# Two more spectral blocks behind the scans, tighter scan spacing in the front, and a rounding moved to GpSimd

## The chip, the cores and the metric

One core of one Trainium2 chip runs the whole kernel. The metric is the device time of one execution in microseconds (us); lower is better. TensorE (PE in the profile) multiplies matrices, VectorE (DVE), ScalarE (ACT) and GpSimd (POOL) work on whole tiles, and SyncE (SP) issues most of the DMAs. All of them run at their own pace, each in the order of its own instruction list, and wait for each other by semaphores. "PEld" is TensorE's loading of weights.

## The reference, cut to what matters

The output mixes softmax attention (32 heads of width 16) and the real part of a two-dimensional Fourier transform of the same input by a gate for each row. Shapes are 2048 rows by 512 columns, all float32.

```python
a = softmax(q @ k.T / 4) @ v            # per head, then @ wo        (32 heads of 16)
b = Cr @ (x @ Wr.T) - Ci @ (x @ Wi.T)   # Cr, Ci: 2048x2048 cosine and sine matrices
g = sigmoid((x * gate_w).sum(-1))
out = g * a + (1 - g) * b
```

## The kernel before

**Arithmetic.** Where exactness is needed, an operand is split into a rounded part and its rest (`hi`, `lo`, type float32r), and a product is three matmul pairs: hi·hi, hi·lo, lo·hi. "Pair" means that `halves_of` (L204) puts two matmuls of 64 rows on the upper and lower half of the array at the same time; a pair is the unit of the orders below (the profile counts its two matmuls singly).

**Scans.** The softmax needs the greatest score of every query before the exponentials. So every pair of heads (16 of them) is first scanned: 64 scans for each pair, 1024 in all (`TOTAL`). A scan multiplies 128 queries by 512 keys and takes the row maximum.

**Three stretches.**
1. The front. It computes the projections q, k, v, wr, wi (each 16 blocks of 12 pairs) and then spectral blocks (each 16 row tiles by three, that is 48 pairs): 16 blocks with the cosine matrix (`ph` 0), then blocks with the sine matrix (`ph` 1). Between the pairs of a product stand the first 740 scans (`FRONT`). `products` and the spectral loop call `beside()` after every pair; it adds 1/pace to a counter and puts a scan in whenever the counter reaches 1. The paces are numbers in the source, one for each part of the front: `PACE, SUMS, BESIDE, PART, SWAP`, in pairs for each scan. Scans in the front are "folded": `scan_folded` writes scores to one of four PSUM banks (L173), ScalarE copies the even ones to SBUF (`fold`, L177), and VectorE adds the odd ones to them and takes the maximum (`fold`, L179, followed by a short read of its accumulator, also L179). Two scans later the same bank is written again, so TensorE then waits if the reader is late.
2. The steps: 512 steps of 16 head pairs by 32 (`PERIODS`). Step by step TensorE computes scores (`qk`, L229: one pair of matmuls into a double bank, one into two single banks), ScalarE takes exponentials (L253 on 1024 columns, L261 twice on 512), and TensorE multiplies them with the values (`pv`, L752). Up to step 284 each step also holds one of the remaining scans. From step `MIX` = 285 on, each step holds "filling" instead (`next(fill)`): the generator `outputs()` yields the spectral blocks that the front left over, 16 steps each, three pairs a step (`spectral`); then `crosses()`, which gets the last `CROSS` = 8 blocks' worth from 14 products of 24 pairs each; then the output projection (`mix_heads`, 9 pairs for each of 16 row tiles, in four steps or in two); and the last parts. In even steps the filling stands ahead of the scores, in odd steps behind them, and both steps' value products are issued together at the end of the even step. So TensorE's order over two steps is: eight value products, scores, the filling of two steps in one piece, scores.
3. A short tail.

**The operands of `crosses()`** are formed on VectorE by `form_unit` (L982 rounds, L983 takes the rest), at steps given by offsets in the table `crossed`; each is loaded seven steps earlier by `begin_unit` on SP's queue, and every form writes over the block that the cross before used. `gather` (L1028, L1029) empties the accumulator after 24 pairs; the additions on the results are GpSimd's, and `finish` stores them.

**The first differences.** In the front, `difference` makes the sums for folded scans from key projections: GpSimd subtracts, ScalarE rounds to `dh`, GpSimd subtracts again, SP stores. `f` = 0 falls into the first 40 us, before the scans begin. `after(n, ...)` puts a call into a list that is run n pairs later, which sets its place in every engine's order.

`ROWS` says at which scan the rows of the next head pair are fetched.

Of the kernel before, what the change touches and what calls it, by code (L numbers as in the profile page):

```python
# [24 lines left out]
NB = S // P  # L25
# [6 lines left out]
PERIODS = 2 * NB  # L32
SCANS = 64
TOTAL = SCANS * NP
LATER = 10
CROSS = 8
EARLY = range(11)
PARTS = {12: 16, 11: 20}
FRONT = SCANS * len(EARLY) + sum(PARTS.values())
PACE, SUMS, BESIDE, PART, SWAP = 2.95, 3.6, 2.72, 2.11, 2.97  # L40
END_PAIR, PART_PAIR = PARTS
SEQ = [(p, i) for p in EARLY for i in range(SCANS)]
SEQ += [(p, i) for p, n in PARTS.items() for i in range(n)]
SEQ += [(p, i) for p in (PART_PAIR, 13, 14, 15, END_PAIR) for i in range(PARTS.get(p, 0), SCANS)]
ROWS = {SCANS * n + 20: p for n, p in enumerate(EARLY[1:])}
ROWS.update({SCANS * len(EARLY) - 60: END_PAIR, SCANS * len(EARLY) - 34: PART_PAIR})
NWARM = 20
MIX = TOTAL - FRONT + 1
HALVED = MIX + NB * (LATER - CROSS)
STEPS = [3, 2, 2, 3, 2, 2, 3, 2, 2, 3]  # L50
TURN = 2 * len(STEPS)
OUT = HALVED + 7 * TURN
SLOW = 5
SCANS_IN = 0
AHEAD = (30, 31, 37, 44)
TURNED = 476
# [10 lines left out]
def build(tc, xT, wqkv, wo, wrT, wiT, cr, ci, ct, gate, out):  # L67
    nc = tc.nc
    with ExitStack() as ctx:
# [200 lines left out]
        with ExitStack() as pf:  # L270
# [11 lines left out]
            def after(n, f, *args):  # L282

                count[0] += 1
                due.append((slots[0] + n, count[0], f, args))
# [75 lines left out]
            for ph, plain, pair in ((0, range(NB - 2), (NB - 2, NB - 1)), (1, range(2, NB), (0, 1))):  # L361
                split_up = [(ph, t, u) for half in range(2) for t in pair for u in (2 * half, 2 * half + 1)]
                whole = [(ph, t, u) for t in plain for u in range(NU)]
                coef += split_up + whole if ph else whole + split_up
            coef = coef[:len(coef) - NU * LATER]
            craw, ready = {}, {}
# [25 lines left out]
            with ExitStack() as px:  # L392
# [48 lines left out]
                def difference(f, c, s):  # L441

                    kept.append(s)
                    if c % 2 == 0:
                        return
                    a, b = kept
                    kept.clear()
                    hi = (ep.tile([P, 512], F32R, tag="gb", name="dh", bufs=1) if f else
                          rp.tile([P, 512], F32R, tag="raw", name="dh"))
                    lo = b.bitcast(F32R)  # L450

                    def store(i, v):
                        nc.sync.dma_start(kf_d[f][:, i, (c - 1) * 512:c * 512], v.bitcast(F32))

                    after(11, nc.gpsimd.tensor_sub, a, a, b)
                    after(16, nc.scalar.copy, hi, a)
                    after(17, nc.gpsimd.tensor_sub, lo, a, hi.bitcast(F32))
                    after(22, store, 0, hi)
                    after(25, store, 1, lo)
# [169 lines left out]
            with ExitStack() as py:  # L629
# [36 lines left out]
                for n, (ph, t, u) in enumerate(coef):  # L666
# [12 lines left out]
                    hi, lo = ready.pop(n)  # L679
# [47 lines left out]
        with ExitStack() as pa:  # L727
# [141 lines left out]

            raws, units = [], [(t, u) for t in range(NB - LATER, NB - CROSS) for u in range(NU)]  # L870
            parts = []
# [37 lines left out]
            crossed, begun, sets, kept = [], {}, {}, {}  # L909

            for n, (left, right) in enumerate(CROSSES):
                crossed += [(TURN * n + at, n, left if f is not None else right, f, u)
                            for at, f, u in ((-8, 0, 0), (-6, None, 0), (-5, None, 1), (-4, None, 2), (-2, None, 3),
                                             (-1, 0, 1), (0, None, 4), (1, None, 5), (2, None, 6), (4, None, 7),
                                             (7, 1, 0), (9, 1, 1))]

            def quarter(f, u, a, b):

# [136 lines left out]
            def crosses():  # L1055

                for n in range(len(CROSSES)):
                    for f in range(2):
                        ps = pair_banks()
                        done = 0  # L1060
                        for u in range(8):
                            left, right = sets[f, u // CS], sets[None, u]
                            q = slice((u % CS) * P, (u % CS + 1) * P)
                            for i, (a, b) in enumerate(((0, 0), (0, 1), (1, 0))):
                                halves_of((ps[:, 0, :], ps[:, 1, :]), left[a][:, q], right[b],
                                          u == 0 and i == 0, u == 7 and i == 2)
                                done += 1
                                if done in [sum(STEPS[:k]) for k in range(1, len(STEPS))]:
                                    yield
                        gather(n, f, ps, now[0] - HALVED)  # L1070
                        yield

# [50 lines left out]
            def outputs():  # L1123

                for t in range(NB - LATER, NB - CROSS):
                    yield from spectral(t)
# [46 lines left out]
            for step in range(NP * PERIODS):  # L1173
                p, i = step // PERIODS, step % PERIODS
# [38 lines left out]
                done = None  # L1213
                for _ in range(min(len(pend), 1) if step < MIX else 0 if step % 2 else 2):
                    done = flush()
# [10 lines left out]
                sum_quarters(step)  # L1226
                crossing(step - HALVED)
                if TURNED <= step < TURNED + CROSS:
                    load_turned(NB - CROSS + step - TURNED)
                if TURNED + 11 <= step < TURNED + 11 + CROSS:  # L1230
                    take_turned(NB - CROSS + step - TURNED - 11)
# [76 lines left out]
```

## Time and profile before

| | us |
|---|---|
| time, median of 3 runs (lowest, highest) | 1734.22 (1733.69, 1735.02) |
| the profiled execution | 1735.44 |
| its span, first to last instruction | 1733.6 |
| front: up to the first wide exponential | 669.4 |
| steps with scans (0 to 287, by the wide exponentials) | 550.2 |
| steps with spectral filling (288 to 319) | 69.9 |
| steps 320 to 511 and the tail | 444.1 |

The granted TensorE clock is 0.999 of full speed over the span. The rows of the profile quoted in the prediction come from five views: the page of the whole execution; windows (busy time of each engine in a stretch, with the number of instructions in brackets); groups of instructions by line in a window; and the timeline, whose rows give the start in us from the span's start, the duration, the engine, the line, what is written from what, how often in sequence, and in brackets the idle time before with the instruction that ended it; and windows for one line alone.

### The profile page before, as it was taken

To read this page: it belongs to the slowest core of one execution; us is meant where nothing else is said; L and a number is where in the kernel's file an instruction comes from. 1 tells how busy PE (TensorE), PEld (TensorE's weight loads), DVE (VectorE), ACT (ScalarE), POOL (GpSimd) and SP (SyncE) were. 2 spreads that over 40 slices of the span, in tenths; PEclk is the share of its full clock that TensorE was granted. 3 is DMA by queue.
4 is the path that set the end of the run, shared out by engine and by line. 5 is a ranking of instruction groups with operands and counts; after the bars stand their busy time and mean duration, and the time that the engine had idled before them with its cause. 6 is when DMAs were issued, how large, how long until landed. Compare 5 with 4: busy or idle time off the path is not lost.

```text
span 1733.6 us, 36853 instructions
## 1 busy us (share of the span) xinstructions
PE 1718.4 (99%) x13560; PEld 1034.1 (60%) x13560; DVE 1149.3 (66%) x2290; ACT 1540.4 (89%) x2554; POOL 744.8 (43%) x893
## 2 busy tenths in 40 slices
PE   8999999999999999999999999999999999999998
PEld 6889888998988786333333333334554444444454
DVE  6688888899999996676676676667133435353243
ACT  5788888888888888999999999999888888888886
POOL 3452234755555762434535455353322334344222
PEclk9999999999999999999999999999999999999999
DMA  7783446643435676256444445354365444455733
GB/s 272 240 318 72 129 137 198 173 117 112 123 112 164 167 160 126 72 130 166 135 110 115 117 117 142 87 140 93 101 148 127 117 115 110 130 142 139 178 108 125
DMA packets 149573, 242.04 MB, mean 140 GB/s; under 512 B 50144, under 2 KB 60880, under 8 KB 142800
## 3 DMA queue, kind: packets, MB, share of 16 engines
q1 hardware_dynamic: 134128, 218.32, 45.5%
q0 software_dynamic: 14688, 20.33, 5.0%
q8 instruction: 106, 1.74, 0.4%
q10 hardware_dynamic: 576, 1.05, 0.2%
q14 instruction: 75, 0.61, 0.1%
HBM read 156.24 MB, written 83.11 MB: 138 GB/s over the span
## 4 chain that ended last, share of the span: by engine, by line
PE 95%; DMA 2%; DVE 1%; SPq 0%; issue 0%; POOL 0%; ACT 0%; DVEq 0%; POOLq 0%; ACTq 0%
PE pvb L752 28%; PE xy L204 25%; PE s L229 19%; PE s L173 11%; PE s L204 8%; PE s L154 4%; DMA raws<-wqkv 0%; DMA q_d<-eh 0%; DMA raws<-xT 0%; DVE fold L179 0%; PE s L549 0%; DVE y L867 0%; SPq L780 0%; DMA b<-o_d 0%; DVE b L348 0%
## 5 line engine op out<-in xcount | busy, mean ns | idle before, releaser
L253 ACT ACTIVATE eb<-s 128x1024 f32<-128x1024 f32 x512 | 571.7, 1117 | 67.0 <-PE s L229 66.9
L261 ACT ACTIVATE e<-s 128x512 f32<-128x512 f32 x1022 | 602.1, 695 | 0.0
L179 DVE CUSTOM_DVE_ANT_0 fold<-s,fold 128x512 f32<-128x512 f32 x740 | 497.8, 690 | 67.7 <-PE s L173 37.2
L177 ACT ACTIVATE fold<-s 128x512 f32<-128x512 f32 x740 | 437.2, 603 | 84.9 <-PE s L173 65.8
L752 PE MATMUL pvb<-eb,va 128*17 128x512 f32 x2052 | 511.5, 597 | 0.3 <-DVE ob L761 0.3
L752 PE MATMUL pvb<-e,va 128*17 128x512 f32 x2044 | 510.7, 597 | 0.0
L156 DVE TENSOR_REDUCE mx<-s 128x2 f32<-128x1024 f32 x284 | 348.0, 1225 | 171.7 <-PE s L154 171.6
L229 PE MATMUL s<-qs,ks 50*128 50x512 f32 x2048 | 435.3, 439 | 0.0
L229 PEld LDWEIGHTS s<-qs,ks 50*128 50x128 f32 x2048 | 210.0, 184 | 371.8 <-ACT eb L253 252.1
L204 PE MATMUL xy<-b,c 64*128 64x512 f32 x2496 | 405.8, 392 | 2.5 <-DVE b L348 1.6
L173 PE MATMUL s<-ks,qs 48*128 48x512 f32 x1480 | 356.7, 403 | 1.8 <-DVE mx L179 1.3
L204 PEld LDWEIGHTS xy<-b,c 64*128 64x128 f32 x2496 | 289.4, 187 | 22.6 <-DVE b L348 2.9
L173 PEld LDWEIGHTS s<-ks,qs 48*128 48x128 f32 x1480 | 194.4, 184 | 46.0 <-DVE mx L179 10.8
L752 PEld LDWEIGHTS pvb<-eb,va 128*17 128x17 f32 x2052 | 71.3, 96 | 193.7 <-issue 184.8
L204 PE MATMUL s<-b,b 64*128 64x512 f32 x1050 | 139.8, 392 | 0.1
L204 PE MATMUL xy<-w,b 64*128 64x512 f32 x768 | 116.8, 392 | 0.0
L154 PE MATMUL s<-ks,qs 48*128 48x512 f32 x568 | 114.9, 395 | 0.1
L204 PEld LDWEIGHTS s<-b,b 64*128 64x128 f32 x1050 | 100.2, 185 | 24.5 <-issue 1.0
L379 POOL TENSOR_TENSOR c<-craw,c 128x512 fp32r<-128x512 f32 x84 | 109.1, 1298 | 6.7
L771 POOL DMA_DIRECT2D r_d<-lc x31 | 17.8, 575 | 214.5 <-DVE lc L770 194.6
L764 POOL DMA_DIRECT2D lc<-ob x124 | 62.8, 513 | 103.7 <-DVE ob L761 90.7
L773 POOL DMA_DIRECT2D rb<-r_d x124 | 60.5, 495 | 106.4 <-DMA r_d<-lc 101.0
(142 smaller groups left out, 1538.8 us busy)
## 6 DMA issues: line engine op xcount, KB each, us to landing
qs<-q_d SPq DMA_DIRECT2D x68, 256.0 KB, 5.7
craw<-cr SPq DMA_DIRECT2D x60, 256.0 KB, 3.5
craw<-ct SPq DMA_DIRECT2D x48, 256.0 KB, 4.9
ks<-k_d SPq DMA_DIRECT2D x42, 256.0 KB, 5.9
kept_None<-sum SPq DMA_DIRECT2D x40, 256.0 KB, 2.4
craw<-kept_None SPq DMA_DIRECT2D x40, 256.0 KB, 3.8
qs<-q_d SPq DMA_DIRECT2D x68, 128.0 KB, 7.1
craw<-ci SPq DMA_DIRECT2D x32, 256.0 KB, 4.3
```

Of the source, the lines that this page charges most:

```text
L154: nc.tensor.matmul(ps[:, j, :], qs[b:b + 48, qb * P:(qb + 1) * P], ks[b:b + 48, c * 512:(c + 1) * 512], start=True, stop=True)
L156: nc.vector.tensor_reduce(mx[p][:, :, qb, c], ps, axis=AX.X, op=ALU.max)
L173: nc.tensor.matmul(ps, qs[b:b + 48, qb * P:(qb + 1) * P], ks[b:b + 48, c * 512:(c + 1) * 512], start=True, stop=True)
L177: nc.scalar.activation(fold[j], ps, AF.Relu)
L179: nc.vector.tensor_tensor_reduce(out=fold[j], in0=ps, in1=fold[j], scale=1.0, scalar=-3.0e38, op0=ALU.add, op1=ALU.max, accum_out=mx[p][:, ...
L204: nc.tensor.matmul(ps[j], lhs[r], rhs[r], start=first, stop=last)
L229: nc.tensor.matmul(pss[j], ks[b:b + 50, kb * P:(kb + 1) * P], qs[b:b + 50, q0:q0 + 512], start=True, stop=True)
L253: nc.scalar.activation(e, ps, AF.Exp, scale=SCALE)
L261: nc.scalar.activation(e[j], pss[j], AF.Exp, scale=SCALE)
L379: sub(lo, raw, hi.bitcast(F32))
L752: nc.tensor.matmul(pvb[r:r + VC, :], va[:, kb, 2 * p + j, :], es[c][j], start=kb == 0, stop=kb == NB - 1, tile_position=(0, r))
L764: nc.gpsimd.dma_start(lc[32 * n:32 * n + 32, :], ob[r + DH:r + VC, :].rearrange("p (s e) -> p s e", e=16))
```

## The change

The number of sine blocks left to the steps (`LATER`) rises from 10 to 12, so the front computes two blocks fewer and `outputs()` two more (`t` = 4 and 5). The number of scans in the front stays 740, and the paces are made tighter to fit them in. To keep the total number of steps, a cross product of 24 pairs now takes 8 steps of three pairs; before it took 10 steps of 3, 2, 2, 3, 2, 2, 3, 2, 2 and 3 pairs. The offsets in `crossed` are compressed from a turn of 20 steps to one of 16. `HALVED`, the step at which the crosses begin, goes from 317 to 349, and `OUT`, where the output projection begins, from 457 to 461. `SLOW` goes from 5 to 3: three row tiles of the output projection instead of five are spread over four steps. The rows of the tenth next pair are fetched 10 scans later. The rounding of `dh` for `f` = 0 goes from ScalarE to GpSimd.

```diff
-LATER = 10
+LATER = 12
 CROSS = 8
+SAVED = 2 * CROSS
-PACE, SUMS, BESIDE, PART, SWAP = 2.95, 3.6, 2.72, 2.11, 2.97
+PACE, SUMS, BESIDE, PART, SWAP = 2.72, 3.1, 2.5, 2.03, 2.85
-ROWS = {SCANS * n + 20: p for n, p in enumerate(EARLY[1:])}
+ROWS = {SCANS * n + (20 if n < 9 else 30): p for n, p in enumerate(EARLY[1:])}
 MIX = TOTAL - FRONT + 1
+OUT = MIX + NB * LATER - SAVED
 HALVED = MIX + NB * (LATER - CROSS)
-STEPS = [3, 2, 2, 3, 2, 2, 3, 2, 2, 3]
-TURN = 2 * len(STEPS)
-OUT = HALVED + 7 * TURN
-SLOW = 5
+SLOW = 3
...
-                    after(16, nc.scalar.copy, hi, a)
+                    after(16, nc.scalar.copy if f else nc.gpsimd.tensor_copy, hi, a)
...
-                crossed += [(TURN * n + at, n, left if f is not None else right, f, u)
-                            for at, f, u in ((-8, 0, 0), (-6, None, 0), (-5, None, 1), (-4, None, 2), (-2, None, 3),
-                                             (-1, 0, 1), (0, None, 4), (1, None, 5), (2, None, 6), (4, None, 7),
-                                             (7, 1, 0), (9, 1, 1))]
+                crossed += [(NB * n + at, n, left if f is not None else right, f, u)
+                            for at, f, u in ((-8, 0, 0), (-6, None, 0), (-5, None, 1), (-4, None, 2), (-2, 0, 1),
+                                             (-1, None, 3), (0, None, 4), (2, None, 5), (3, None, 6), (4, None, 7),
+                                             (6, 1, 0), (7, 1, 1))]
...
-                        done = 0
                         for u in range(8):
...
-                                done += 1
-                                if done in [sum(STEPS[:k]) for k in range(1, len(STEPS))]:
-                                    yield
+                            if u < 7:
+                                yield
                         gather(n, f, ps, now[0] - HALVED)
                         yield
```

In the orders below the changed kernel's lines stand one lower than the old ones, `w_1220` of the old is `w_1234` of the new, and x2 is one pair.

**ScalarE and GpSimd near the end of the first key and query blocks** (about 24 to 33 us of the profile; `b` are the split columns of x that the next products read, `raws` the loaded ones, `eh` a rounded projection, `tx` an emptied accumulator). ScalarE before:

```order
L471 COPY tx<-s_469 128x512
L297 CAST dh<-s 128x512
L347 CAST b_227<-raws 128x512
L297 CAST eh<-s 128x512
L347 CAST b_229<-raws 128x512
L471 COPY tx<-xy 128x512
```

ScalarE now:

```order
L470 COPY tx<-s_469 128x512
L346 CAST b_227<-raws 128x512
L296 CAST eh<-s 128x512
L346 CAST b_229<-raws 128x512
L470 COPY tx<-xy 128x512
```

GpSimd now, where before the CAST was missing:

```order
L296 TENSOR_TENSOR el<-s,eh 128x512 x4
L296 TENSOR_TENSOR s<-s 128x512
L296 CAST dh<-s 128x512
L296 TENSOR_TENSOR s<-s,dh 128x512
L296 TENSOR_TENSOR el<-s,eh 128x512 x4
```

The rounding has left ScalarE's list, where it stood ahead of four roundings of x, and now stands between GpSimd's two subtractions.

**TensorE in the value projection** (a stretch with the pace `BESIDE`; L204 a pair of the product, L173 a scan). Before:

```order
L204 MATMUL xy<-w_1220,b_231 128x512 x2
L204 MATMUL xy<-w_1221,b_231 128x512 x2
L173 MATMUL s<-ks,qs 128x512 x2
L204 MATMUL xy<-w_1220,b_232 128x512 x2
L204 MATMUL xy<-w_1220,b_233 128x512 x2
L204 MATMUL xy<-w_1221,b_233 128x512 x2
L173 MATMUL s<-ks,qs 128x512 x2
```

Now, a little further on:

```order
L203 MATMUL xy<-w_1235,b_229 128x512 x2
L203 MATMUL xy<-w_1234,b_230 128x512 x2
L172 MATMUL s<-ks,qs 128x512 x2
L203 MATMUL xy<-w_1234,b_231 128x512 x2
L203 MATMUL xy<-w_1235,b_231 128x512 x2
L203 MATMUL xy<-w_1234,b_232 128x512 x2
L172 MATMUL s<-ks,qs 128x512 x2
L203 MATMUL xy<-w_1234,b_233 128x512 x2
L203 MATMUL xy<-w_1235,b_233 128x512 x2
L172 MATMUL s<-ks,qs 128x512 x2
```

Runs of two and three pairs between scans alternate now, where three were the rule. Over the whole front TensorE's list holds 2016 pairs and 740 scans before, 1920 pairs and 740 scans now; 71, 70 and 71 scans stand in the v, wr and wi projections before, 77 in each now.

**TensorE in the crosses** (L229 the scores of a step, L204 the filling of two steps). Before:

```order
L229 MATMUL s_18595<-qs,ks 128x512 x2
L229 MATMUL s_18599<-qs,ks 128x512
L229 MATMUL s_18600<-qs,ks 128x512
L204 MATMUL s_18419<-b_18475,b_18405 128x512 x2
L204 MATMUL s_18419<-b_18474,b_18406 128x512 x2
L204 MATMUL s_18419<-b_18523,b_18405 128x512 x2
L204 MATMUL s_18419<-b_18524,b_18405 128x512 x2
L204 MATMUL s_18419<-b_18523,b_18406 128x512 x2
L229 MATMUL s_18620<-qs,ks 128x512 x2
```

Now:

```order
L228 MATMUL s_19339<-qs,ks 128x512 x2
L228 MATMUL s_19343<-qs,ks 128x512
L228 MATMUL s_19344<-qs,ks 128x512
L203 MATMUL s_19349<-b_19189,b_19143 128x512 x2
L203 MATMUL s_19349<-b_19190,b_19143 128x512 x2
L203 MATMUL s_19349<-b_19189,b_19144 128x512 x2
L203 MATMUL s_19349<-b_19219,b_19143 128x512 x2
L203 MATMUL s_19349<-b_19220,b_19143 128x512 x2
L203 MATMUL s_19349<-b_19219,b_19144 128x512 x2
L228 MATMUL s_19368<-qs,ks 128x512 x2
```

Two steps hold four or five pairs of a cross before and six now. The number of such pieces of filling is 114 before and after; 11 of them hold nine pairs before (row tiles of the output projection in two steps), 13 now.

## The prediction

> **What bounds the kernel now.** I read the page first, then windows by stretch, then timelines inside them. The page says that TensorE is never idle, which would make every pair equally dear wherever it stands:
>
> ```profile
> PE 1718.4 (99%) x13560; PEld 1034.1 (60%) x13560; DVE 1149.3 (66%) x2290; ACT 1540.4 (89%) x2554; POOL 744.8 (43%) x893
> ```
>
> The windows (us, then busy time of PE, PEld, DVE, ACT, POOL, each with its count) tell two regimes apart: the front (v projection, part of the cosine blocks) and the steps (spectral filling; steps 320 onward up to the output projection):
>
> ```profile
> 121.40:183.50 62.10, 62.10 (x528) 56.78 (x526) 54.21 (x156) 52.55 (x99) 14.51 (x12) 1.00 0.33 88
> 420.00:460.00 40.00, 40.00 (x339) 35.29 (x337) 36.74 (x111) 33.88 (x60) 20.39 (x22) 1.00 0.36 108
> 1219.60:1289.50 69.90, 69.90 (x574) 36.68 (x572) 20.87 (x38) 62.30 (x97) 20.63 (x34) 1.00 0.50 130
> 1289.50:1594.20 304.70, 304.70 (x2339) 143.31 (x2340) 130.45 (x209) 271.26 (x419) 106.45 (x149) 1.00 0.50 125
> ```
>
> PE reads full in all four, but in the front 264 pairs stand in 62.1 us (528 matmuls, 0.235 us each pair) with weights loading 91% of the time, and in the steps weights load 47 to 52%. What the steps wait for is in the timeline of two steps with six filling pairs (TensorE, then ScalarE's wide exponentials):
>
> ```profile
> 1254.66 0.61 PE L752 MATMUL pvb<-eb,va 128*17 128x512 f32 x2
> 1256.50 0.73 PE L229 MATMUL s<-qs,ks 50*128 50x512 f32 x4
> 1257.07 0.63 PE L204 MATMUL s<-b,chi 64*128 64x512 f32 x4
> 1257.54 0.39 PE L204 MATMUL s<-b,clo 64*128 64x512 f32 x2
> 1257.77 0.62 PE L204 MATMUL s<-b,chi 64*128 64x512 f32 x4
> 1258.22 0.39 PE L204 MATMUL s<-b,clo 64*128 64x512 f32 x2
> 1258.45 0.65 PE L229 MATMUL s<-qs,ks 50*128 50x512 f32 x4
> 1254.55 1.04 ACT L253 ACTIVATE eb<-s 128x1024 f32<-128x1024 f32 x1
> 1257.04 1.03 ACT L253 ACTIVATE eb<-s 128x1024 f32<-128x1024 f32 x1 [0.47 <-PE s L229]
> 1258.92 1.04 ACT L253 ACTIVATE eb<-s 128x1024 f32<-128x1024 f32 x1
> ```
>
> The first exponential waits for the scores behind the value products (0.47 us idle), the second starts as soon as ScalarE is through. So two steps last 4.37 us: a stretch of TensorE (value products and scores, 2.49 us), then a stretch of ScalarE (1.88 us), under which the filling runs, 1257.07 to 1258.45.
>
> **The steps: three pairs in each.** The crosses had four or five pairs in two steps. Here are two steps with four:
>
> ```profile
> 1467.14 1.09 PE L204 MATMUL s<-b,b 64*128 64x512 f32 x8
> 1464.61 1.04 ACT L253 ACTIVATE eb<-s 128x1024 f32<-128x1024 f32 x1
> 1468.98 1.04 ACT L253 ACTIVATE eb<-s 128x1024 f32<-128x1024 f32 x1
> ```
>
> Again 4.37 us. Over many steps (us, ScalarE's time in L253, number of them), first three pairs a step, then 2.4 but for the last steps:
>
> ```profile
> 1219.60:1289.50 69.90, 33.09 (x32) 1.00 0.50 130
> 1289.50:1569.60 280.10, 132.64 (x128) 1.00 0.50 126
> ```
>
> 69.90/32 = 2.184 and 280.10/128 = 2.188 us a step. I therefore cost the 96 pairs that move into the steps at **0**; their cover is ScalarE's stretch. What a moved block issues besides (four loads of coefficients, a load and a store of `y` on SP, four splits and two updates on VectorE) is in the first of these windows as well, which is two such blocks: VectorE has 20.87 of 69.9 us there, and the steps are no longer for any of it. In the front the same splits were GpSimd's and the emptying ScalarE's, so both are relieved. It is just enough: nine pairs, as in the output projection, don't fit. In ScalarE's timeline there, the second step of such a two takes 2.57 us, where it took 1.88 above, and ScalarE waits for scores in it too:
>
> ```profile
> 1598.35 1.03 ACT L253 ACTIVATE eb<-s 128x1024 f32<-128x1024 f32 x1 [0.47 <-PE s L229]
> 1600.92 1.02 ACT L253 ACTIVATE eb<-s 128x1024 f32<-128x1024 f32 x1 [0.56 <-PE s L229]
> ```
>
> 0.69 us for three pairs too many, 0.23 each. If the cover were gone, the moved pairs would cost that, 22 us. The output projection has 13 such pieces of nine pairs now against 11: 2 x 0.69 = **+1.4 us**. The number of steps is the same, so nothing else is added at the end; VectorE in the crosses forms 12 operands in 35 us instead of 43.75, and from 130.45/304.7 = 43% busy comes to 54% at most. Its last operands are wanted two steps (4.4 us) after they are due, at the least.
>
> **The front: two blocks less.** What one pair takes is read where 12 stand in a row; the scans between pairs from the cosine part:
>
> ```profile
> 25.33 2.88 PE L204 MATMUL s<-b,w 64*128 64x512 f32 x24
> 399.88 0.43 PE L173 MATMUL s<-ks,qs 48*128 48x512 f32 x2
> 400.12 0.66 PE L204 MATMUL xy<-b,c 64*128 64x512 f32 x4
> 400.58 0.43 PE L173 MATMUL s<-ks,qs 48*128 48x512 f32 x2
> 400.46 0.69 DVE L179 CUSTOM_DVE_ANT_0 fold<-s,fold 128x512 f32<-128x512 f32 x1
> 401.12 0.69 DVE L179 CUSTOM_DVE_ANT_0 fold<-s,fold 128x512 f32<-128x512 f32 x1
> ```
>
> A pair's own record is 0.39 us, so 11 distances fill 2.88 - 0.39, 0.227 each. Two pairs and a scan take 400.58 - 399.88 = 0.70, so a scan takes 0.246. The front loses 2 x 48 = 96 pairs and no scan: 96 x 0.227 = **-21.8 us**; by the mean over all slots (0.236 in the v projection: 62.10 over 192 pairs and 71 scans) it would be -22.7.
>
> That holds if the scans, now closer, don't make TensorE wait. Groups by line in the cosine part:
>
> ```profile
> L204 PE MATMUL xy<-b,c 64*128 64x512 f32 x230 | 38.6, 392 | 0.0
> L179 DVE CUSTOM_DVE_ANT_0 fold<-s,fold 128x512 f32<-128x512 f32 x55 | 37.0, 691 | 3.4 <-PE s L173 1.3 <-ACT fold L177 0.5
> L173 PE MATMUL s<-ks,qs 48*128 48x512 f32 x109 | 25.8, 404 | 0.0
> ```
>
> 115 pairs and 54.5 scans would take 39.5 us by the slot prices; they took 40.0, so with VectorE at 36.74/40 = 92% TensorE lost 1.2%. At the new pace 2.03 a scan comes every 2.03 x 0.227 + 0.246 = 0.707 us, against 40/54.5 = 0.734 measured; the timeline above, at 0.70, shows that folds keep up (0.66 apart where one was late). The v, wr and wi projections hold 77 scans over 192 pairs now, 62.5 us by the slots; VectorE's 54.21 us of work grow by six folds of 0.67 (37.0/55) to 58.2, or 93%: the load of the cosine part today. There ten of 16 blocks also put an addition of 0.69 us on VectorE, and a fold behind it comes late. Bounds of the new waits: 0, and 0.3 us for some 30 such additions, **9 us**. I take **+2.0**, near the lower end, since the stretch that already runs at this load loses 0.5 us in 40.
>
> **The start: the rounding on GpSimd.** TensorE stalls around 28 us, since the split columns of x come late (TensorE, ScalarE, VectorE, GpSimd):
>
> ```profile
> 28.44 0.51 PE L204 MATMUL xy<-b,c 64*128 64x512 f32 x2 [0.23 <-ACT b L347]
> 29.83 0.96 PE L204 MATMUL xy<-b,c 64*128 64x512 f32 x6 [0.88 <-DVE b L348]
> 31.52 2.53 PE L204 MATMUL xy<-b,c 64*128 64x512 f32 x16 [0.73 <-DVE b L348]
> 27.25 0.62 ACT L297 CAST dh<-s 128x512 fp32r<-128x512 f32 x1 [2.17 <-POOL s L297]
> 23.82 0.68 DVE L348 TENSOR_TENSOR b<-raws,b 128x512 fp32r<-128x512 f32 x1
> 28.42 3.65 DVE L348 TENSOR_TENSOR b<-raws,b 128x512 fp32r<-128x512 f32 x3 [2.62 <-ACT b L347]
> 27.95 1.27 POOL L297 TENSOR_TENSOR s<-s,dh 128x512 fp32r<-128x512 f32 x1 [0.73 <-ACT dh L297]
> ```
>
> ScalarE stands 2.17 us for GpSimd's subtraction, with four roundings of x queued behind. These 24 matmuls are 12 pairs; they could have begun 0.23 earlier and end at 34.05, where at 0.227 each and 0.39 for the last 2.9 us would do for the 5.84 that they take. 3.0 us is the most that can go. Without the rounding ScalarE is 2.7 us earlier (2.17 and its own 0.5). But three of VectorE's subtractions took 3.65 us there while GpSimd worked, against 0.68 for one alone, so they may be the next to come late. Bounds: 0 and -3.0; I take **-2.2**. GpSimd itself is later by the 0.6 us of a rounding, ahead of stores that only the scans read, later on.
>
> [...]
>
> **The sum.** -21.8 + 2.0 - 2.2 + 1.4 = -20.6 against the profiled execution's 1735.44 (span 1733.6): 1714.8. That execution lies 1.2 above the median 1734.22, so the forecast is **1713.6**. At the good ends (-22.7, 0, -3.0, +1.4) it is 1709.9, at the bad ones (-21.8, +9, 0, +1.4) 1722.8.
>
> **The rivals.**
> 1. The front gives back half. VectorE, at 93%, can't take additions and folds at this spacing; 9 us or a little more return: 1718 to 1727. For it: VectorE's share; against it: folds at 0.66 us.
> 2. The moved pairs cost in the steps what they save in the front: 96 x 0.23 = 22 back, about 1735. For it: PE's 99%, and that nine pairs overrun the cover at once; against it: 2.184 beside 2.188 us. [...]
> 3. Slower: the left operands of the crosses come late. A form writes over the block that the cross before read, and the lead of the third (`(1, 0)`) falls from three steps to two. If VectorE lags by more than those 4.4 us, TensorE waits for a rounding and a subtraction (0.42 and 0.82 us, groups below) at each of 4 x 7 left operands: 35 us, so 1749. Against it: VectorE half idle there.
>
> ```profile
> L983 DVE TENSOR_TENSOR b<-craw,b 128x512 fp32r<-128x512 f32 x37 | 30.4, 821 | 1.3
> L982 DVE CAST b<-craw 128x512 fp32r<-128x512 f32 x37 | 15.4, 417 | 5.9 <-PE s L204 5.9
> ```
>
> **How the numbers follow.** Chances: the forecast (1709.5 to 1718) 0.67; rival 1 0.17; rival 2 0.06; rival 3 0.05; still faster, below 1709.5, because the front's other waits shrink too, 0.05. A range from 1709.5 to 1722.5 holds the forecast and most of rival 1, about 8 in 10. A difference of 0.2% (3.5 us) is about what a measurement can tell from none: faster than that 0.89 (forecast, rival 1, still faster), the same 0.06 (rival 2), slower 0.05.
>
> **What would show it.** In the changed profile the first wide exponential should stand near 669.4 - 22 = 647 us; at 655 or later rival 1 holds, with idle time of TensorE's L173 behind `mx` L179. Two steps of crosses should still last 4.37 us; 4.6 or more means rival 2, and idle time of L204 behind VectorE's `b` in the crosses rival 3. ScalarE's idle time before `dh` near 27 us should be gone, and the stalls at 28 to 32 us mostly. The prediction is wrong if the front ends above 660 us or the steps grow by more than 5 us.

## The result and the profile after

| us | before | changed |
|---|---|---|
| time, median (lowest to highest) of six runs each | 1735.01 (1733.69 to 1738.4) | 1720.82 (1718.53 to 1722.92) |
| the profiled execution | 1735.44 | 1718.53 |
| its span | 1733.6 | 1716.7 |
| front: up to the first wide exponential | 669.4 | 651.5 |
| first 288 steps | 550.1 | 549.5 |
| steps 288 to 447 | 350.1 | 350.0 |
| steps 448 to 511 | 146.3 | 147.8 |

The changed kernel takes 0.9915 of the time, 95% interval 0.9902 to 0.9928. This ratio is of the means, which differ by 14.8 us; the medians differ by 14.2. The median lies in the predicted range but 7.2 us above the 1713.6 forecast. The profiled executions differ by 16.9 us; the changed kernel's was the fastest of its six.

Most of the missing time is in the front. It was to end 22 us earlier and ended 17.9 earlier. To see where, I cut TensorE's front into stages, from the start of one pair to the start of another, and took off the prediction's prices: 0.227 us a pair and 0.246 a scan. What is left I call the stage's waits (at the start, loads and stalls; later, mostly scans that stand for a bank). "Spectral" counts pairs from the first cosine block on.

| stage | before, us | scans | waits | changed, us | scans | waits |
|---|---|---|---|---|---|---|
| start, to pair 96 (x columns, gate) | 37.55 | 0 | 15.8 | 35.62 | 0 | 13.8 |
| q | 41.84 | 18.5 | 1.9 | 42.69 | 20.5 | 2.2 |
| k | 45.81 | 47 | 1.6 | 47.77 | 52 | 2.3 |
| v | 62.04 | 71 | 1.0 | 64.61 | 77 | 2.1 |
| wr | 63.27 | 71 | 2.2 | 65.52 | 77 | 3.0 |
| wi | 62.20 | 70 | 1.4 | 65.58 | 76 | 3.3 |
| spectral, first 576 pairs | 201.54 | 271 | 4.1 | 205.00 | 282 | 4.9 |
| spectral, the rest | 155.19 | 191.5 | 5.5 | 124.67 | 155.5 | 5.6 |

From q on the waits grew from 17.6 to 23.4 us, by 5.8; the forecast had +2.0. The start gave 1.9 instead of 2.2.

The windows answer those shown of the kernel before (first column the stretch, then busy us of TensorE, weight loading, VectorE, ScalarE and GpSimd with their instructions, then granted clock, DMA share, GB/s). Changed kernel: the v projection, a piece of the cosine part, spectral filling, crosses.

```profile
126.10:190.70 64.60, 64.60 (x542) 55.68 (x539) 58.16 (x167) 55.88 (x106) 14.42 (x13) 1.00 0.33 81
420.00:460.00 40.00, 40.00 (x338) 36.34 (x336) 36.80 (x113) 34.63 (x63) 22.60 (x24) 1.00 0.37 109
1201.00:1271.00 70.00, 70.00 (x578) 37.10 (x576) 14.33 (x24) 62.39 (x98) 20.35 (x34) 1.00 0.41 92
1334.40:1579.40 245.00, 245.00 (x2018) 129.57 (x2018) 133.87 (x212) 218.31 (x336) 92.10 (x128) 1.00 0.59 148
```

VectorE has 58.16 of 64.60 us in the v projection, 90%, and 36.80 of 40, 92%, in the cosine part. The crosses now keep it busy for 133.87/245 = 55% of the time, and they are no longer per step than before.

Which waits grew is in the view that groups waits by who waited for whom (engine, what, line, releaser; then us in total, times, longest), over the v, wr and wi projections. Before (125.2 to 312.7 us):

```profile
DVE fold L179 <- PE s L173: 17.5, 69, 0.4
DVE fold L179 <- ACT fold L177: 5.2, 16, 0.9
PEld s L173 <- DVE mx L179: 3.4, 12, 1.0
PEld s L173 <- ACT fold L177: 1.6, 5, 0.6
```

The changed kernel (126.1 to 321.8 us):

```profile
DVE fold L178 <- ACT fold L176: 8.4, 28, 1.2
PEld s L172 <- DVE mx L178: 7.9, 33, 0.7
DVE fold L178 <- PE s L172: 6.0, 31, 0.2
PEld s L172 <- ACT fold L176: 2.7, 6, 0.6
```

Before, VectorE mostly waited for scores, that is, it was early. Now it is late: TensorE's scans wait for its maxima 33 times instead of 12, 7.9 us instead of 3.4. (These are waits of weight loading, which starts ahead of its matmuls, at 150.53 us for a scan whose matmuls start at 150.76, so not every one is lost time: in the start below, at 31.39 us, loading waited 1.38 us where the matmuls stood 0.96.) And VectorE itself waits longer for ScalarE's copy of the other half, 8.4 us instead of 5.2.

The timeline of the steps (start, duration, engine, line, what) shows two steps with six pairs of crosses, TensorE and then ScalarE's wide exponentials, in the changed kernel:

```profile
1452.86 1.55 PE L203 MATMUL s<-b,b 64*128 64x512 f32 x12
1452.83 1.02 ACT L252 ACTIVATE eb<-s 128x1024 f32<-128x1024 f32 x1 [0.48 <-PE s L228]
1454.70 1.04 ACT L252 ACTIVATE eb<-s 128x1024 f32<-128x1024 f32 x1
1457.20 1.03 ACT L252 ACTIVATE eb<-s 128x1024 f32<-128x1024 f32 x1 [0.48 <-PE s L228]
```

1457.20 - 1452.83 = 4.37 us for two steps with 12 matmuls, which is what eight took before.

The start, same view, in the changed kernel (TensorE, ScalarE, VectorE, GpSimd):

```profile
28.01 2.43 PE L203 MATMUL xy<-b,c 64*128 64x512 f32 x20
31.39 0.73 PE L203 MATMUL xy<-b,c 64*128 64x512 f32 x4 [0.96 <-DVE b L347]
26.56 1.14 ACT L346 CAST b<-raws 128x512 fp32r<-128x512 f32 x2
29.57 0.69 DVE L296 TENSOR_TENSOR s<-xy,tx 128x512 f32<-128x512 f32 x1 [1.18 <-POOL s L296]
30.18 1.15 DVE L347 TENSOR_TENSOR b<-raws,b 128x512 fp32r<-128x512 f32 x1
26.89 0.95 POOL L296 CAST dh<-s 128x512 fp32r<-128x512 f32 x1
27.93 1.61 POOL L296 TENSOR_TENSOR s<-s,dh 128x512 fp32r<-128x512 f32 x1
```

ScalarE no longer stands for GpSimd and has all four roundings done by 27.7 us. But the last split of x is VectorE's, and ahead of it VectorE now waits 1.18 us for a buffer. Its next sum takes one of the three in the ring `raw`, which still holds what GpSimd's second subtraction reads until 29.54. So three stalls, with 0.23, 0.88 and 0.73 us of idle time, became one with 0.96. What is gained is mostly what stands behind the last stall: four matmuls (0.73 us) from 31.39, where before it was sixteen (2.53 us) from 31.52.

### The profile page after: what moved, and what is told of

The parts are those of the page before. It is cut to its first block, busy times and chain, and to the rows that moved or that the text cites. A ratio compares the mean times of both kernels' runs of the same rounds, so it can differ in the third digit from the quotient of the medians.

```text
span 1716.7 us, 36848 instructions
## 1 busy us (share of the span) xinstructions
PE 1702.1 (99%) x13560; PEld 1027.3 (60%) x13560; DVE 1158.0 (67%) x2310; ACT 1535.5 (89%) x2548; POOL 726.6 (42%) x875
## 3 DMA queue, kind: packets, MB, share of 16 engines
q8 instruction: 106, 1.74, 0.5%
## 4 chain that ended last, share of the span: by engine, by line
PE 94%; DMA 2%; DVE 1%; issue 1%; ACT 1%; POOL 1%; SPq 0%; DVEq 0%; POOLq 0%; ACTq 0%
PE pvb L751 28%; PE xy L203 23%; PE s L228 18%; PE s L172 11%; PE s L203 9%; PE s L153 4%; DVE fold L178 1%; DMA raws<-wqkv 0%; ACT fold L176 0%; DMA q_d<-eh 0%; DMA raws<-xT 0%; PE s L548 0%; DVE y L866 0%; POOL s L296 0%; DMA k_d<-eh 0%
## 5 line engine op out<-in xcount | busy, mean ns | idle before, releaser
L228 PEld LDWEIGHTS s<-qs,ks 50*128 50x128 f32 x2048 | 214.7, 184 | 349.3 <-ACT eb L252 242.2
L228 PE MATMUL s<-qs,ks 50*128 50x512 f32 x2048 | 417.3, 434 | 0.0
L203 PE MATMUL xy<-b,c 64*128 64x512 f32 x2304 | 377.7, 392 | 1.2 <-DVE b L347 1.0
L172 PE MATMUL s<-ks,qs 48*128 48x512 f32 x1480 | 366.3, 406 | 2.1 <-DVE mx L178 0.7
L203 PEld LDWEIGHTS xy<-b,c 64*128 64x128 f32 x2304 | 264.4, 187 | 17.3 <-DVE b L347 1.4
L172 PEld LDWEIGHTS s<-ks,qs 48*128 48x128 f32 x1480 | 199.8, 184 | 57.7 <-DVE mx L178 17.8
L751 PEld LDWEIGHTS pvb<-eb,va 128*17 128x17 f32 x2052 | 71.3, 96 | 191.5 <-issue 183.0
L203 PE MATMUL xy<-w,b 64*128 64x512 f32 x768 | 123.3, 392 | 0.0
L153 PE MATMUL s<-ks,qs 48*128 48x512 f32 x568 | 114.7, 394 | 0.0
L378 POOL TENSOR_TENSOR c<-craw,c 128x512 fp32r<-128x512 f32 x76 | 99.8, 1313 | 6.1
```

The costliest lines, as they stand in the source:

```text
L153: nc.tensor.matmul(ps[:, j, :], qs[b:b + 48, qb * P:(qb + 1) * P], ks[b:b + 48, c * 512:(c + 1) * 512], start=True, stop=True)
L172: nc.tensor.matmul(ps, qs[b:b + 48, qb * P:(qb + 1) * P], ks[b:b + 48, c * 512:(c + 1) * 512], start=True, stop=True)
L203: nc.tensor.matmul(ps[j], lhs[r], rhs[r], start=first, stop=last)
L228: nc.tensor.matmul(pss[j], ks[b:b + 50, kb * P:(kb + 1) * P], qs[b:b + 50, q0:q0 + 512], start=True, stop=True)
L378: sub(lo, raw, hi.bitcast(F32))
L751: nc.tensor.matmul(pvb[r:r + VC, :], va[:, kb, 2 * p + j, :], es[c][j], start=kb == 0, stop=kb == NB - 1, tile_position=(0, r))
```

## The experiments

The waits given below are counted as in the table.

### 1. The paces alone

The kernel before, with nothing but the new paces. (`ROWS`, which the expectation names, was left as it was.)

```diff
-PACE, SUMS, BESIDE, PART, SWAP = 2.95, 3.6, 2.72, 2.11, 2.97
+PACE, SUMS, BESIDE, PART, SWAP = 2.72, 3.1, 2.5, 2.03, 2.85
```

> The kernel before with the new paces (and ROWS) alone; LATER stays 10, so pairs and steps are unchanged. Theory A (the closer scans make TensorE wait, above all in the k, v, wr and wi projections, behind VectorE's additions): the projections lose what they lose in the changed kernel, 2.1, 3.0 and 3.3 us beyond the slot prices in v, wr and wi against 1.0, 2.2 and 1.4 before; the front ends 4 to 6 us later than before, about 1739 to 1741 us in all. Theory B (the waits come from the shorter front, not from the paces): no change, 1735 us.

Measured: 1740.97 us, 1.0037 of the kernel before (1.0024 to 1.0049), 5.8 us more. The waits are those of the changed kernel in every stage, within 0.3: v 2.1, wr 3.0, wi 3.6, first 576 spectral pairs 4.9, 23.6 in all. So the loss comes from the spacing alone and from nothing that the moved blocks do. (The first wide exponential came 7.6 us later, and 1.7 of that was there at pair 96, where in the profiled execution TensorE's granted clock was at half for about 3.4 us, 0.50 from 32 to 34 us and 0.65 from 34 to 36; see the last section.)

### 2. No additions on VectorE

In the projections ten of 16 blocks add two halves on VectorE. Here the changed kernel gives all these additions to GpSimd.

```diff
-                    if beds and t % 3 and t < NB - 1:
+                    if False:
```

> The changed kernel with every addition of the v, wr and wi projections on GpSimd (ScalarE empties the second half too); before, VectorE did 10 of 16. Theory A: VectorE's load there falls from 89 to about 79 percent and the waits of the scans with it; the v, wr and wi stretches get 4 to 6 us shorter together, about 1715 to 1717 us in all. Theory C (ScalarE is what comes late, or the spacing itself): ScalarE gets 30 more instructions of 0.6 us, no gain or a loss, 1721 to 1726 us.

Measured: 1719.46 us, 0.9909 (0.9894 to 0.9924). The waits fall from 23.4 to 22.4 only: v by 1.1 and wi by 0.8, but the rest stays or rises a little. That misses the 1715 to 1717 us of theory A. The groups by line from 126.1 to 321.8 us tell why (count, then busy us, mean ns, idle time before and its releasers); these are the v, wr and wi projections of the changed kernel, and within about 3 us those of the kernel with the edit. The changed kernel:

```profile
L178 DVE CUSTOM_DVE_ANT_0 fold<-s,fold 128x512 f32<-128x512 f32 x231 | 156.3, 689 | 21.5 <-ACT fold L176 8.4 <-PE s L172 6.0 <-PE xy L203 1.4
L296 ACT ACTIVATE ty<-xy 128x512 f32<-128x512 f32 x18 | 11.0, 612 | 0.0
```

With the additions on GpSimd:

```profile
L178 DVE CUSTOM_DVE_ANT_0 fold<-s,fold 128x512 f32<-128x512 f32 x233 | 159.4, 691 | 32.1 <-ACT fold L176 14.8 <-PE s L172 6.8 <-PE xy L203 0.5
L296 ACT ACTIVATE ty<-xy 128x512 f32<-128x512 f32 x48 | 29.5, 614 | 0.0
```

In this program GpSimd's addition takes both halves from ScalarE's copies (`va<-tx,ty`, where VectorE's is `va<-tx,xy`), so ScalarE empties the second accumulator too: 30 copies `ty` more, 18.5 us. VectorE is relieved, 163.28 us busy instead of 174.06, and then waits for ScalarE, 14.8 us instead of 8.4. The edit moved part of the lateness from one engine to the other; it could not tell how much of it is VectorE's.

### 3. The old paces in the projections

The scans that the projections don't take go into the cosine part.

```diff
-PACE, SUMS, BESIDE, PART, SWAP = 2.72, 3.1, 2.5, 2.03, 2.85
+PACE, SUMS, BESIDE, PART, SWAP = 2.95, 3.6, 2.72, 1.9, 2.85
```

> The changed kernel with the paces of before in the projections (2.95, 3.6, 2.72) and 1.9 in place of 2.03 in the cosine and sine part, which then takes 25 scans more. Theory A: the projections lose 4 to 5 us less; the cosine part, where two pairs and a scan take 0.70 us and a fold at least 0.66, loses 2 to 6 us more; 1719 to 1723 us in all. Theory D (the front has room for folds at any spacing, and only additions are dear): the cosine part loses under 1 us more, about 1716.5 us in all.

Measured: 1724.18 us, 0.9939 (0.9926 to 0.9951). The projections' waits are back at those of before (v 1.0, wr 2.2, wi 1.7), but the first 576 spectral pairs, with 301 scans instead of 282, wait 11.6 us instead of 4.9, and those behind them 8.3 instead of 5.6. The projections lose 4.7 us less, as theory A has it; the spectral part loses 9.4 more, above its 2 to 6, and the time is above its range. The window of the cosine part:

```profile
420.00:460.00 40.00, 39.99 (x329) 34.12 (x327) 37.41 (x115) 34.84 (x62) 20.15 (x22) 1.00 0.36 101
```

VectorE goes from 36.80 to 37.41 us of 40, while TensorE does 329 matmuls where the changed kernel did 338. So 19 scans more in the first 576 pairs cost 6.7 us of waits; the changed kernel's division of the scans is better than this one.

### 4. Which engine is late

The changed kernel and the kernel before, with VectorE taking only 256 of 512 columns of each folded maximum, and then with ScalarE copying only 256 as well. Half of the keys are left out of the front's maxima.

```diff
-nc.scalar.activation(fold[j], ps, AF.Relu)
+nc.scalar.activation(fold[j][:, :256], ps[:, :256], AF.Relu)
...
-nc.vector.tensor_tensor_reduce(out=fold[j], in0=ps, in1=fold[j], ...
+nc.vector.tensor_tensor_reduce(out=fold[j][:, :256], in0=ps[:, :256], in1=fold[j][:, :256], ...
```

The sums named in the expectations run from q to the 576th spectral pair. The halved maxima in the changed kernel:

> The changed kernel with half of the work of every folded maximum on VectorE: it adds and reduces 256 of the 512 columns, so half of the keys are left out of the maxima of the front's scans. Everything else, ScalarE's copies too, stays. Waits are counted over the slot prices (0.227 a pair, 0.246 a scan) from the q projection to the end of the cosine and sine blocks' scans: 17.8 us in the changed kernel, 12.2 in the kernel before. Theory V (the closer scans wait because VectorE is too slow for them): the maxima fall from 0.67 to about 0.4 us, VectorE to some 60% busy, and the waits to 12 us or less; first wide exponential at 646 or earlier. Theory S (they wait because ScalarE's copies into the fold come late, VectorE being fast enough): 16 to 18 us stay, first wide exponential near 651.

The halved copies too:

> The same, and ScalarE copies only the first 256 columns of the other half of the scores (the same half of the keys is left out). Theory V: nothing further, within 1 us of the kernel with the halved maxima. Theory S: this is the kernel in which the waits fall, to 12 us or less. If both fall together only here, both engines' lateness mattered.

The kernel before with halved maxima:

> The kernel before with the same halved maxima (256 of 512 columns; half of the keys left out). It gives the waits that have nothing to do with VectorE's rate at the wider spacing. Theory V: they fall from 12.2 us to what the changed kernel with halved maxima has, within 1.5 us, so that the whole difference between the two kernels' waits is VectorE's; the difference of the first wide exponentials is then 21 to 23 us. Theory S: they stay near 12, and the difference of the first wide exponentials stays near 18.

And with both:

> The kernel before with halved maxima on VectorE and halved copies on ScalarE (half of the keys left out). Waits over the slot prices from the q projection to the end of the first of the two parts of the spectral blocks were 12.2 us before and 17.8 changed; with halved maxima 10.2 and 12.5; with both halved 7.2 in the changed kernel. If the closer scans cost nothing but lateness of VectorE and ScalarE, both halved gives 6 to 8 us here too, within 1 us of the changed kernel, and the first wide exponentials lie 22 to 24 us apart (96 pairs at 0.227, and the start), this one at 660 to 663. If closer scans cost something else besides (waits for loads, or TensorE's own), the changed kernel's 7.2 is 2 us or more above this one's, which then has 5 or less and an exponential at 659 or earlier.

Measured once each: 1712.25 us (halved maxima), 1704.94 (both) for the changed kernel, 1731.26 and 1726.7 for the kernel before.

| waits, us | as it was | halved maxima | both halved |
|---|---|---|---|
| before, q to 576th spectral pair | 12.2 | 10.2 | 6.7 |
| changed, q to 576th spectral pair | 17.8 | 12.5 | 7.2 |
| before, q to the end of the front | 17.6 | 14.3 | 8.7 |
| changed, q to the end of the front | 23.4 | 17.4 | 9.7 |
| difference, whole front | 5.8 | 3.1 | 1.0 |
| first wide exponential, before / changed | 669.4 / 651.5 | 665.7 / 646.1 | 661.2 / 638.4 |

The groups by line from 126 to 322 us, and TensorE's own waits for its two readers there (the v, wr and wi projections and 4 to 7 us behind them), with halved maxima and whole copies:

```profile
L178 DVE CUSTOM_DVE_ANT_0 fold<-s,fold 128x256 f32<-128x256 f32 x235 | 99.5, 424 | 76.8 <-PE s L172 57.6 <-ACT fold L176 16.8 <-PE xy L203 1.3
L176 ACT ACTIVATE fold<-s 128x512 f32<-128x512 f32 x236 | 139.1, 604 | 18.5 <-PE s L172 15.1
PEld s L172 <- ACT fold L176: 3.6, 6, 1.5
PEld s L172 <- DVE mx L178: 0.6, 1, 0.6
```

And with both halved:

```profile
L178 DVE CUSTOM_DVE_ANT_0 fold<-s,fold 128x256 f32<-128x256 f32 x238 | 100.7, 424 | 75.4 <-PE s L172 67.6 <-ACT fold L176 3.3 <-PE xy L203 2.3
L176 ACT ACTIVATE fold<-s 128x256 f32<-128x256 f32 x238 | 91.7, 387 | 57.3 <-PE s L172 51.0 <-DVE g L591 0.6
PEld s L172 <- ACT fold L176: 1.1, 2, 0.9
PEld s L172 <- DVE mx L178: 0.4, 1, 0.4
```

A maximum now takes 0.424 us, and VectorE idles 76.8 us ahead of them, yet 16.8 us of that is still waiting for ScalarE's copies; with these at 0.387 us it is 3.3. The waits of TensorE's weight loading agree: for the maxima they fall from 7.9 us to 0.6; for the copies they are 3.6, and 1.1 when these are halved too. VectorE's lateness alone does not explain the difference of 5.8 us: halved maxima take 2.7 of it away, halved copies a further 2.1, and 1.0 stays. (The copies were not halved alone, so how the 4.8 divides between the engines is shown for this order only, from one execution of each kernel.) Theory V as written (VectorE alone) falls short, and so does theory S. The last expectation's first case came in: both halved, the two kernels' waits agree within 1 us (6.7 and 7.2), and the first wide exponentials lie 661.2 - 638.4 = 22.8 us apart. Of this 2.0 are the start (pair 96 at 38.2 and 36.2 us, and about 1.0 of that is a stretch of half clock in the kernel before, 0.50 from 32 to 34 us; see the last section), so 20.8 are left from pair 96 on, 1.0 less than the price of the pairs. The v projection also bears out the prices: with both halved, 192 pairs and 77 scans take 62.77 us, where 192 x 0.227 + 77 x 0.246 = 62.5.

### 5. The rounding: back on ScalarE, alone, and with a buffer of its own

Back on ScalarE in the changed kernel, and alone in the kernel before (the same line the other way):

```diff
-                    after(16, nc.scalar.copy if f else nc.gpsimd.tensor_copy, hi, a)
+                    after(16, nc.scalar.copy, hi, a)
```

> The changed kernel with the rounding of the first differences back on ScalarE. Theory A: the stall near 28 us returns; the first wide exponential comes 1.5 to 2 us later than in the changed kernel (653.0 to 653.5 us), about 1722.5 us in all. Theory E (the rounding doesn't matter; the 1.5 us at the start are chance of the first loads): no change, 1720.8 us.

> The kernel before with the rounding of the first differences on GpSimd alone. Theory A: the stretch from the last key block's start to the end of the gate sums falls from 9.1 to about 7.6 us, 1733 to 1734 us in all. Theory H (what the rounding saves in one place the half-clock window takes back in most runs): 10.1 us and a window near 32 us in the profile, 1735 us in all.

Measured: 1720.76 us (0.9926, 0.9913 to 0.9939) without it, 1733.88 us (0.9991, 0.9982 to 1.0) with it alone. By the runs it is worth between nothing and about 3 us, which decides neither between theories A and E nor between A and H. With the rounding back on ScalarE the three stalls are back (0.50, 0.88 and 0.72 us). The first wide exponential of that kernel, at 660.1 us, can't be used: its profiled execution was the slowest of its five, 1726.32 us, with half clock in two places (the granted clock is 0.72 from 28 to 40 us and 0.84 from 570 to 580).

By the profiles pair 96 starts at 35.92 us with the rounding alone and at 37.55 before, 1.6 earlier, and 1.9 earlier in the changed kernel. But pair 72, which comes ahead of the rounding, already started at other times: at 24.52 us with the rounding alone, at 25.33 before, at 25.29 in the changed kernel. From pair 72 to pair 96 it is 12.2 us in the kernel before, with and without halved maxima; 11.4 or 11.5 in three kernels with the rounding on GpSimd (alone, and the two of experiment 4); and 10.3 in the changed kernel, whose one stall lasted 0.96 us where it lasted 1.95 or 1.96 in those three. So the rounding is worth 0.8 to 1.9 us. (With it alone, the stretch that the expectation names fell from 9.1 to 8.7 us, not to 7.6.)

The third variant takes `dh` out of the ring `raw`, so that VectorE's sum finds a buffer:

```diff
-                           rp.tile([P, 512], F32R, tag="raw", name="dh"))
+                           ep.tile([P, 512], F32R, tag="el", name="dh", bufs=4))
```

> The changed kernel with the rounded difference dh in the ring of the rounded rests (tag el, four buffers) instead of the ring of three that also holds the sums s. Theory F (with the rounding on GpSimd, VectorE's next sum waits 1.2 us for a buffer that GpSimd still reads, and the TensorE stall of 1.3 to 2.1 us behind it also brings a half-clock window of 3.4 us in some runs): the wait on GpSimd before VectorE's s is gone, the stretch from 28 us to the end of the gate sums falls from 7.6 (without such a window) or 10.1 us (with it) to 6.5, no window near 32 us, 1718 to 1719.5 us in all. [...]

Measured: 1720.07 us (0.991, 0.9896 to 0.9923), which can't be told from the changed kernel and misses the 1718 to 1719.5 of theory F. The wait for the buffer is gone and pair 96 comes at 35.18 instead of 35.62, but the gain ends at the first scan. Timeline of TensorE and of SP's queue in this kernel:

```profile
59.29 0.40 PE L172 MATMUL s<-ks,qs 48*128 48x512 f32 x1
62.27 0.47 PE L172 MATMUL s<-ks,qs 48*128 48x512 f32 x1 [2.58 <-DMA ks<-kf_d]
55.37 0.45 SPq L115 DMA_DIRECT2D ks<-kf_d  x1
```

And in the changed kernel:

```profile
59.77 0.40 PE L172 MATMUL s<-ks,qs 48*128 48x512 f32 x1
60.66 0.46 PE L172 MATMUL s<-ks,qs 48*128 48x512 f32 x1 [0.49 <-PE s L172]
53.79 0.48 SPq L115 DMA_DIRECT2D ks<-kf_d  x1
```

TensorE is earlier, the last load of the first scanned keys is issued 1.6 us later, and the scan behind it stands 2.58 us for it. Why SP was later is not settled.

### 6. Both edits together

`dh` in the other buffer and all additions on GpSimd:

> The run before with every addition of the v, wr and wi projections on GpSimd as well. Both effects add if they are what they seem (about 1 us from the additions, 1.3 to 3 us from the buffer): 1717 to 1718.5 us, below the changed kernel by more than the interval. If the additions' gain was chance: the same as e5.

Measured: 1719.44 us (0.9903, 0.9889 to 0.9916), above the 1717 to 1718.5 that were expected; pair 96 at 34.14 us, and 2.39 us between the first scans' starts. With experiment 2's 1719.46 it is the lowest median of a whole computation, but its interval overlaps the changed kernel's, so it can't be called faster than that.

## Why the prediction was right, and where it was not

- **The moved pairs, 0 in the steps.** Right. Two steps of crosses take 4.37 us with six pairs, and steps 288 to 447 last 350.0 us against 350.1. Rival 2 needed 22 us there. Rival 3 did not come either: in the view of waits over the crosses (1334.4 to 1579.4 us) no matmul waits for VectorE's `b`.
- **Two more pieces of nine pairs, +1.4.** Right: 147.8 - 146.3 = 1.5.
- **96 pairs out of the front, -21.8.** Right as a price, to within 1.0: with the readers' work halved, the kernels are 20.8 us apart from pair 96 to the first wide exponential, and the changed one waits 1.0 longer. (The waits are counted at the same prices, so the two say the same thing; what bears the prices out is the v projection of experiment 4.)
- **New waits of the scans, +2.0.** This is the term that was mis-sized: 5.8, inside its bounds of 0 and 9. The step that failed is "near the lower end, since the stretch that already runs at this load loses 0.5 us in 40". It took VectorE's share as the measure of waiting, and a short stretch as the sample. At 92% those 40 us wait 1.2%, and the 576 pairs around them 4.1 of 201.5 us, 2.0%; at 90% the v projection of the changed kernel waits 2.1 us in 64.6, 3.3%. The term was worked out for v, wr and wi, where 3.8 of the 5.8 arose; 1.0 came in q and k and 0.9 in the spectral part, which it left out. ScalarE's lateness had no term in the sum at all, though the view of waits before the change already showed VectorE waiting 5.2 us for it. In the order of experiment 4, 2.7 of the 5.8 go with VectorE's maxima and 2.1 with ScalarE's copies; 1.0 is not explained. The share that the additions have can't be told, since moving them loaded ScalarE.
- **The rounding, -2.2.** The mechanism was right, the size too large in most executions: -2.2 was an estimate between the bounds of 0 and -3.0 that no run shows, and the profiles show 0.8 to 1.9 (experiment 5). The changed kernel's profiled execution is at the upper end. Next late is VectorE's split of x, as the prediction feared, but first of all for a buffer (1.18 us of waiting). Side by side both engines took longer: GpSimd's rounding 0.95 us beside VectorE's splits, while its other roundings of that size take 0.61 (the row of `c` below, cosine part of the changed kernel, where VectorE is 92% busy, mostly with maxima), and VectorE's subtraction 1.15 us against 0.68 alone. What makes them longer is not shown.

```profile
L377 POOL CAST c<-craw 128x512 fp32r<-128x512 f32 x10 | 6.1, 612 | 16.9 <-PE xy L203 16.5 <-PE s L172 0.4
```

- **What it comes to.** The four terms as measured, -21.8 + 5.8 - 1.9 + 1.5, make -16.4; steps 0 to 287 were 0.6 shorter, which nothing had forecast, and the spans differ by 16.9. The profiled execution was forecast at 1714.8 and took 1718.5, 3.7 more: nearly all of it the new waits. The median misses by 3.5 more, since the forecast took the profiled execution to lie 1.2 above the median, and the changed kernel's lies 2.3 below. The median, 1720.82, lies above the stretch of 1709.5 to 1718 that was given to the forecast itself and inside rival 1's 1718 to 1727; it is in the range because the range took in most of rival 1, not because the term was right. The front ended at 651.5, between the forecast's 647 and the 655 from which rival 1 was to hold. So rival 1's mechanism was at work at about two thirds of its size, with ScalarE as a partner that it did not name.
- **Open.** The medians differ by 14.2 us and the profiled executions by 16.9. The changed kernel's profiled execution lies 2.3 us below its median and the one before 0.4 above, which is the 2.7 between the two. What sets single executions apart is not shown; the half clock of the last section is one thing that differs between them.

## What to carry to other kernels

The busy share of VectorE did not tell here how long TensorE would wait for it (1.2% of the time at 92%, 3.3% at 90%). Look in the view of waits at how early its instructions are, and at every engine in the chain behind the buffer (here copy, then maximum), and give each a term. To find out which of two readers is late, halve the work of each alone and of both, in the old kernel and in the new (the copies alone were left out here); moving work to a third engine may load the other one instead (in experiment 2 ScalarE, by 18.5 us). A wait that was removed here uncovered the next one in order on the same path (in experiment 5 pair 96 came 0.44 us earlier, and then a scan stood 2.58 us for its keys), so follow that path up to the first point where a load sets the time, before the gain is counted.

## What the runs showed of the hardware that was not expected

After TensorE's stall near 30 us the granted clock fell in some executions and not in others. The timeline of the kernel of experiment 3 (old paces in the projections), with 32 matmuls of the gate (L548) behind the stall:

```profile
31.71 0.73 PE L203 MATMUL xy<-b,c 64*128 64x512 f32 x4 [1.77 <-DVE b L347]
32.37 5.34 PE L548 MATMUL s<-raws,gw 128*32 128x512 f32 x32
```

And of the kernel before with the rounding alone on GpSimd, where the same matmuls are L549:

```profile
31.69 0.73 PE L204 MATMUL xy<-b,c 64*128 64x512 f32 x4 [1.96 <-DVE b L348]
32.35 3.64 PE L549 MATMUL s<-raws,gw 128*32 128x512 f32 x32
```

Same place, about the same stall, 5.34 against 3.64 us for the same 32 matmuls. Windows of 34 to 40 us, the third number from the end being the granted clock (1.00 is full speed); the first kernel:

```profile
34.00:40.00 6.00, 6.00 (x46) 2.57 (x40) 2.33 (x4) 2.38 (x7) 1.27 (x1) 0.84 0.31 116
```

and the second:

```profile
34.00:40.00 6.00, 6.00 (x52) 3.47 (x46) 2.33 (x3) 3.14 (x8) 2.29 (x2) 1.00 0.34 128
```

Five of the thirteen profiled executions show it near 31 to 34 us; neither of the two compared at the top does. In two the 32 gate matmuls took 1.7 us longer. In two others it fell on the 16 product matmuls ahead of them, 3.65 and 3.49 us (2.53 before the change), about 1.0 us. In the fifth it lasted twice as long and cost about 2.4 us. The stalls ahead of it were single ones of 1.74 and 1.77 us, and three in a row of 2.1 to 2.6 us in all. Single stalls of 1.95 and 1.96 us passed without it in three executions, and so did three in a row of 1.84 us in the kernel before and the 2.58 us at the first scans in experiment 5. So about the same stall cost 1.7 us extra in one execution and nothing in another.

How long it lasted can be worked out from the granted clock of 28 to 40 us, as far as it was at half, 0.50, the least that the windows of 2 us show. It is 0.86 in four of the five (experiments 1, 2 and 3, and the kernel before with both halved), which makes (1 - 0.86) x 12 / 0.5 = 3.4 us, and 0.72 in the fifth (the rounding back on ScalarE), 6.7 us. The length of the stall alone did not decide it: behind 1.74 and 1.77 us the clock fell, behind 1.95, 1.96 and 2.58 us it did not. What decides it is not shown.
